# Top-32 attention with two MLPs on one core: leaky ReLU as one parametric ReLU on ScalarE

## The chip, the cores and the metric

The kernel runs on one core of a Trainium2 chip. The metric is device time in microseconds (us), from the first to the last instruction of the program; the median of several executions is given. The engines are TensorE (PE, with PEld for its weight loads), VectorE (DVE), ScalarE (ACT), GpSimd (POOL) and SyncE (SP), which issues most DMAs.

## What is computed

Attention over 4 batches, 8 heads, 576 positions and a head size of 64, in which each query keeps its 32 largest scores; then two MLPs on the 2304 tokens, 512 to 2048 to 512 each. The first one has a leaky ReLU with slope 0.01, the second one a SiLU.

```python
def _moe_ref(x, w_in, w_out):
    h = x @ w_in
    g = np.maximum(0.01 * h, h)
    return (g @ w_out).astype(np.float32)
...
attn_out = _attn_ref(q, k, v)          # softmax over the 32 largest scores of a row
x = attn_out.transpose(0, 2, 1, 3).reshape(B * S, H * D)
x = _moe_ref(x, w_in, w_out)
return _moe2_ref(x, w_in2, w_out2)     # h * sigmoid(h) in place of the leaky ReLU
```

## The kernel before

The 2304 tokens are 18 blocks of 128. Blocks 4 and 13 hold the last 64 tokens of two batches each; the other blocks lie in one batch. A block has four pairs of heads, 72 pairs in all. Everything that a matrix product takes is scaled by a power of two and split into two float16 parts, a high one and a low one (value minus high part), so that a product is three passes of float16.

**Attention**, for each pair: `scores` on PE; `chain`, eight steps for each of two heads on DVE (four MAX8 at lines 479 and 490, three MATCH_REPLACE8 at line 488, and at line 482 a product of the exponentials with the mask, whose two inputs lie in SBUF); `s_copy` and `exps` on ACT (lines 512 and 503); `p_hi` on ACT (517), `p_lo` on POOL (523), `p_transpose` by DMA from SP; `pv` on PE (549). Keys and values of a batch and pair are loaded, scaled and split shortly before the first block that uses them, which is block 0, 4, 9 or 13 (lines 316 to 385).

**The layers**, for each block and layer, in four chunks of 512 columns: `h_quantum` on PE (line 640, 12 matmuls into one of two PSUM tiles); in the first layer `g1_a` on ACT (lines 653 and 654: relu(h), and relu(-0.01 h)) and `g1_b` on POOL (659: the first minus the second); in the second layer `g2_a`, a Tanh on ACT (672), and `g2_b` on DVE (677); then in both `g_hi` on ACT (683), `g_lo` on POOL (688), `g_transpose` by DMA from SP (692), and `o_quantum` on PE (706, 12 matmuls).

**Weights** arrive as 64-bit floats and are decoded to float32 (lines 213 to 232), scaled (261 to 265) and split (275 and 281) while the first blocks run.

**Order.** Each engine works off its instructions in the order of issue. Every step is registered at a position with `at(...)`, 16 positions for a pair of heads, and at the end all steps are issued by position; steps at the same position keep the order in which they were registered. A chunk of layer one has its matmuls at `g1 + QP[i]`, its other steps `OG1` positions later, and `o_quantum` 20 positions later. `OG1` holds the offsets of `g1_a`, `g1_b`, `g_hi`, `g_lo` and `g_transpose`. Within a pair the two exponentials are at positions 8 and 13, the masked products at 14 and 15.

**Buffers.** Tiles of one tag take a fixed number of buffers in turn, and a new tile waits until the last reader of the tile that had its buffer is done. Tag "f" has seven buffers of float32 (loads of q, k and v, both Relu results, Tanh results and others), tag "hl" three for pairs of high and low parts, tag "gT" three for transposed chunks.

Of the kernel before, what the change touches and what calls it, by code (L numbers as in the profile page):

```python
# [14 lines left out]
AF = mybir.ActivationFunctionType  # L15
ALU = mybir.AluOpType
# [2 lines left out]
NEG = -3.0e38  # L19
POS = 16  # L20

# Positions of issue: 16 a pair of heads of a block, relative to the pair's first.
QP = (5, 11, 20, 27)
OK = (-44, -37, -33, -33, -22, -22, -21, -14, -12)
OV = (-5, -2, 7, 11, 13, 15, 17, 25)
# [3 lines left out]
OA = (-7, -20, 7, 5, 8, 13, 17, 17, 23, 28)  # L29
ON = (20, 21, 33, 34, 36, 37)  # L30
OX = (38, 39, 39, 40, 44)
OG1 = (5, 7, 9, 11, 16)
OG2 = (6, 6, 6, 15, 18)
OY = (47, 51, 53, 60, 65)
OO = 52
# [25 lines left out]
def topk_attention_moe_moe2_kernel(  # L61
# [8 lines left out]
    moe2_w_out: bass.AP,  # L70
    out: bass.AP,
):
    """Top-32 attention and two MLPs, as one pipeline over blocks of 128 tokens.

    Every float32 operand of a matrix product is scaled by a power of two, taken from its norm, and
    split into two float16 parts (hi + lo), so that the products run at one pass per pair of parts
    and accumulate in float32.
    """
    nc = tc.nc
    B, H, S, D = q.shape  # L80
    DM = moe_w_in.shape[0]
# [17 lines left out]
    ones = wp.tile([128, 128], F32, name="ones")  # L99
# [4 lines left out]
    w_all = wp.tile([128, (4 * NWP + 1) * 2 * WP], F16, name="w_all")  # L104
# [3 lines left out]
    blocks = []  # L108
# [10 lines left out]
    for s in range(NS):  # L119
        blk, p = divmod(s, NP)  # L120
# [5 lines left out]
    def at(s, p, fn, *args):  # L126
        cal[POS * s + p].append((fn, args))

    def f_tile(shape, name, dt=F32):
        return mp.tile(shape, dt, tag="f", name=name, bufs=NF)  # L130
# [24 lines left out]
        nc.tensor.matmul(out=ps, lhsT=ones, rhs=ss)  # L155
        return ps

# [1 line left out]
    # A pair of chunks is 128 rows of 1024 elements: columns of the first matrix of a layer, two rows  # L159
    # of blocks of the second. Pair c of tensor i ends up as (hi | lo) in slot 8 i + c of w_all. Its  # L160
    # float32 values, before the tensor's norm is known, lie one slot further on, and the float64 ones
    # and the scratch of their decoding in slots that are not used yet.
    w_ss = {}
    w_tmp = {}
    w_bits = [w.bitcast(I32) for w in w_src]
# [21 lines left out]
        return LOAD3[c] if i == 3 and c < 6 else OW[i][0] + OW[i][1] * c  # L187

    def w_rows(i, c, o, n):
        """n elements of each row of pair c, from its element o on, as pairs of 32-bit words."""  # L190
        if i in (0, 2):
            kk, h = divmod(c, DFF // WP)
            o += h * WP
            return w_bits[i][kk * 128:(kk + 1) * 128, 2 * o:2 * (o + n)]
        kk, o = divmod(2 * c * DM + o, DM)
        if n <= DM:
            return w_bits[i][kk * 128:(kk + 1) * 128, 2 * o:2 * (o + n)]
        return w_bits[i][kk * 128:(kk + 2) * 128, :].rearrange("(k p) d -> p k d", p=128)

    def w_load(i, c, o, n):  # L200
        if n == 256:
            t = f_tile([128, 2 * n], "wraw", I32)
        else:
            t = w_raw_at(i, c).bitcast(I32)
        dst = t.rearrange("p (k d) -> p k d", k=2) if n > DM and i % 2 else t
        nc.sync.dma_start(out=dst, in_=w_rows(i, c, o, n))
        w_tmp[i, c, o] = t
# [93 lines left out]
        w_scale["u2"] = a[:, 1:2]  # L301
        w_scale["o"] = a[:, 2:3]

# [1 line left out]
    raw = {}  # L305
    kT = {}
    vt = {}
# [123 lines left out]
        )  # L431
        qT[blk, hf] = t

# [1 line left out]
    st = defaultdict(dict)  # L435

    def scores(s):
# [152 lines left out]
        dst = x_f[blk][:, 256 * hf:256 * hf + 256].rearrange("p (h d) -> p h d", d=D)  # L590
        nc.gpsimd.tensor_tensor(out=dst, in0=st.pop(("t2", blk)), in1=r, op=ALU.mult)

# [1 line left out]
    xs = {}  # L594
    xT = {}
    act_f = {}
# [33 lines left out]
    hp = {}  # L630
    gf = {}
# [15 lines left out]
            del xT["xy"[layer], blk]  # L647

    def g1_a(blk, i):
        t = f_tile([128, 512], "g1p")  # L650
        t2 = f_tile([128, 512], "g1n")
        h = hp.pop((0, blk, i))
        nc.scalar.activation(out=t, in_=h, func=AF.Relu)
        nc.scalar.activation(out=t2, in_=h, func=AF.Relu, scale=-0.01)  # L654
        gf[0, blk, i] = (t, t2)

    def g1_b(blk, i):
        t, t2 = gf[0, blk, i]
        nc.gpsimd.tensor_tensor(out=t, in0=t, in1=t2, op=ALU.subtract)  # L659
        gf[0, blk, i] = t  # L660

    def u2_make(blk):
# [54 lines left out]
        for p0, p1, b, t0 in blocks[blk]:  # L717
            nc.scalar.dma_start(out=out[b * S + t0:b * S + t0 + p1 - p0, :], in_=t[p0:p1])

# [1 line left out]
    at(-5, 0, lambda: nc.vector.memset(ones, 1.0))  # L721
    at(-5, 0, lambda: make_identity(nc, ident))

# [18 lines left out]
    for s in range(NS):  # L742
        blk, p = divmod(s, NP)
# [22 lines left out]
    for blk in range(NB):  # L766
        g1 = G1.get(blk, POS * (NP * blk + 6))
        g2 = G2.get(blk, POS * (NP * blk + 12))
        for i in range(NCH):
            for o, fn in zip(OG1, (g1_a, g1_b)):  # L770
                at(0, g1 + QP[i] + o, fn, blk, i)
            at(0, g1 + QP[i], h_quantum, 0, blk, i)
            at(0, g1 + LAGO[0] + QP[i], o_quantum, 0, blk, i)
            at(0, g2 + QP[i], h_quantum, 1, blk, i)
            for o, fn in zip(OG2, (g2_a, g2_b)):
                at(0, g2 + QP[i] + o, fn, blk, i)
            at(0, g2 + LAGO[1] + QP[i], o_quantum, 1, blk, i)
            for layer, g, og in ((0, g1, OG1), (1, g2, OG2)):
                for o, fn in zip(og[2:], (g_hi, g_lo, g_transpose)):
                    at(0, g + QP[i] + o, fn, layer, blk, i)  # L780
        at(0, g1 + OY[0], y_ready, blk)
        for o, fn in zip(OY, (a_square, a_scales, a_hi, a_lo, a_transpose)):
            at(0, g1 + o, fn, ("y", blk))
        at(0, g2 - 1, u2_make, blk)
        at(0, g2 + OO, o_store, blk)
# [47 lines left out]
```

## Time and profile before

| | |
|---|---|
| median of 3 runs | 1168.95 us (1168.84 to 1169.19) |
| the profiled execution's own time, its span | 1169.7 us |
| busy: PE, DVE, POOL, ACT | 991.2, 1034.7, 846.0, 801.1 us |
| instructions | 18519 |

The profiled execution is one more execution; its time is its span, from the first to the last instruction, and nothing lies around it. Busy times are sums over the whole span, which holds stages of different kinds: decoding of weights at the start, attention and layers side by side, and the last layers alone at the end.

### The profile page before, as it was taken

How to read it: one execution, taken by the hardware profiler on the slowest of the kernel's cores; microseconds unless marked ns; L12 is line 12 of the kernel's file. 1: busy time of each engine (PE TensorE's matmuls, PEld its weight loads, DVE VectorE, ACT ScalarE, POOL GpSimd, SP SyncE). 2: the span in 40 equal slices, each digit the busy share in tenths (PEclk: the TensorE clock that was granted, in tenths of full speed). 3: DMA queues.
4: the chain of work that ended last, by engine and by line, in shares of the span. 5: the costliest groups of instructions: out<-in, count | busy, mean ns of one | idle time of the engine just before them, and what ended most of it. 6: DMA issues, size and time to landing. Idle time of an engine off the chain costs nothing.

```text
span 1169.7 us, 18519 instructions
## 1 busy us (share of the span) xinstructions
PE 991.2 (85%) x6024; PEld 494.6 (42%) x6024; DVE 1034.7 (88%) x2020; ACT 801.1 (68%) x1250; POOL 846.0 (72%) x1097
## 2 busy tenths in 40 slices
PE   2332366378899999999998999999999999999998
PEld 2221233133345544444444444444555444444443
DVE  4999999998999999999999999999999999996000
ACT  7787888787786657576786667577666666574332
POOL 2376788499888877677788777688877777775441
PEclk9555568589999999999999999999999999999999
DMA  9945646534766455564766455566746464664322
GB/s 346 305 130 168 195 146 163 151 73 98 155 143 143 100 117 117 112 135 96 173 158 139 107 118 117 120 146 162 139 92 133 108 143 94 127 119 101 72 64 64
DMA packets 458114, 157.48 MB, mean 135 GB/s; under 512 B 440864, under 2 KB 449056, under 8 KB 455968
## 3 DMA queue, kind: packets, MB, share of 16 engines
q1 hardware_dynamic: 455392, 151.57, 55.2%
q10 hardware_dynamic: 2624, 4.72, 1.2%
q8 instruction: 47, 0.77, 0.3%
q14 instruction: 51, 0.42, 0.1%
HBM read 47.71 MB, written 4.72 MB: 45 GB/s over the span
## 4 chain that ended last, share of the span: by engine, by line
DVE 37%; POOL 17%; PE 15%; issue 15%; ACT 11%; DMA 4%; SPq 1%; POOLq 0%; ACTq 0%; DVEq 0%
DVE w L488 10%; DVE m L490 8%; PE acc L706 7%; DVE e L482 7%; PE h L640 6%; DVE m L479 4%; POOL ph L523 3%; DVE w_all L232 3%; POOL g1p L659 3%; POOL ghl L688 3%; ACT e L503 2%; DVE g2t L677 2%; DVE w_all L220 2%; PE pv L549 1%; POOL w_all L281 1%
## 5 line engine op out<-in xcount | busy, mean ns | idle before, releaser
L706 PE MATMUL acc<-w_all,gT 128*128 128x512 f16 x1728 | 398.0, 380 | 21.1 <-DMA gT<-ghl 9.2
L640 PE MATMUL h<-w_all,xT 128*128 128x512 f16 x1728 | 401.7, 383 | 14.5 <-DMA xT<-xhl 6.3
L490 DVE MAX8 m<-w 128x8 f32<-128x576 f32 x432 | 308.4, 742 | 0.0
L640 PEld LDWEIGHTS <-xT 128*128 128x128 f16 x1728 | 169.8, 99 | 219.8 <-issue 17.3
L706 PEld LDWEIGHTS <-gT 128*128 128x128 f16 x1728 | 164.6, 99 | 215.0 <-issue 17.9
L488 DVE MATCH_REPLACE8 w<-m,w 128x576 f32<-128x576 f32 x288 | 211.1, 738 | 0.0
L523 POOL TENSOR_TENSOR ph<-e,ph 128x1152 f16<-128x1152 f32 x72 | 171.8, 2386 | 24.0 <-ACT ph L517 21.7
L482 DVE SCALAR_TENSOR_TENSOR e<-sb,m,e 128x576 f32<-128x576 f32 x144 | 174.9, 1234 | 3.3 <-ACT e L503 3.3
L659 POOL TENSOR_TENSOR g1p<-g1p,g1n 128x512 f32<-128x512 f32 x72 | 96.7, 1342 | 57.4 <-ACT g1n L654 56.6
L677 DVE SCALAR_TENSOR_TENSOR g2t<-g2t,h 128x512 f32<-128x512 f32 x72 | 48.6, 675 | 94.7 <-ACT g2t L672 93.6
L503 ACT ACTIVATE e<-sb,nb,u 128x576 f32<-128x576 f32 x144 | 120.9, 859 | 5.3 <-POOL nb L495 4.3
L688 POOL TENSOR_TENSOR ghl<-g2t,ghl 128x512 f16<-128x512 f32 x72 | 87.1, 1210 | 47.3 <-ACT ghl L683 47.1
L549 PE MATMUL pv<-vt,pT 128*128 128x128 f16 (+3 forms) x1600 | 112.2, 214 | 9.7 <-DMA pT<-ph 9.7
L688 POOL TENSOR_TENSOR ghl<-g1p,ghl 128x512 f16<-128x512 f32 x72 | 93.9, 1304 | 36.3 <-ACT ghl L683 35.8
L517 ACT ACTIVATE ph<-e 128x1152 f16<-128x1152 f32 x72 | 83.5, 1160 | 51.4 <-DVE e L482 51.4
L241 PE MATMUL gram<-w_all 128*128 128x128 bf16 x256 | 32.4, 292 | 97.6 <-DVE w_all L232 94.6
L683 ACT ACTIVATE ghl<-g1p 128x512 f16<-128x512 f32 x72 | 45.3, 630 | 92.5 <-POOL g1p L659 89.0
L549 PEld LDWEIGHTS <-pT 128*128 128x128 f16 (+3 forms) x1600 | 87.1, 102 | 48.6 <-DMA pT<-ph 11.7
L488 DVE MATCH_REPLACE8 w<-m,S 128x576 f32<-128x576 f32 x144 | 106.2, 743 | 0.0
L479 DVE MAX8 m<-S 128x8 f32<-128x576 f32 x144 | 102.7, 749 | 0.8 <-PE S L448 0.8
L512 ACT ACTIVATE sb<-S 128x1152 f32<-128x1152 f32 x72 | 80.8, 1123 | 31.8 <-DVE w L488 31.7
L448 PE MATMUL S<-kT,qT 128*128 128x64 f16 (+3 forms) x640 | 90.7, 302 | 12.2 <-ACT sb L512 11.7
(94 smaller groups left out, 1242.4 us busy)
## 6 DMA issues: line engine op xcount, KB each, us to landing
w_all<-in_moe_w_in_dram SPq DMA_DIRECT2D x16, 1024.0 KB, 5.4
w_all<-in_moe_w_out_dram SPq DMA_DIRECT2D x14, 1024.0 KB, 5.2
rawk<-in_k_dram SPq DMA_DIRECT2D x16, 256.0 KB, 3.0
rawq<-in_q_dram SPq DMA_DIRECT2D x32, 128.0 KB, 3.0
rawv<-in_v_dram SPq DMA_DIRECT2D x16, 256.0 KB, 3.0
out_dram<-of ACTq DMA_DIRECT2D x16, 256.0 KB, 2.6
gT<-ghl SPq DMA_TRANSPOSE x144, 2.8
wraw<-in_moe_w_out_dram SPq DMA_DIRECT2D x8, 256.0 KB, 3.3
```

The source lines that it names most:

```text
L448: nc.tensor.matmul(out=t[p0:p1, o:o + k1 - k0], lhsT=lhs, rhs=kt[:, k0:k1], start=(x == 0), stop=(x == 1),)
L479: nc.vector.max(m[:, 0], s_ps(s, h))
L482: nc.vector.scalar_tensor_tensor(out=d["e"][:, h], in0=d["sb"][:, h], scalar=m[:, 3, 7:8], in1=d["e"][:, h], op0=ALU.is_ge, op1=ALU.mult, ...
L488: nc.vector.match_replace(w, m[:, step // 2], src, NEG)
L490: nc.vector.max(m[:, step // 2], w)
L503: nc.scalar.activation(out=d["e"][:, h], in_=d["sb"][:, h], func=AF.Exp, scale=d["u"], bias=d["nb"][:, h:h + 1])
L523: nc.gpsimd.tensor_tensor(out=d["ph"][:, 1], in0=d["e"].rearrange("p h k -> p (h k)"), in1=d["ph"][:, 0], op=ALU.subtract)
L549: nc.tensor.matmul(out=o[p0:p1, h, p % 2, 0:n], lhsT=l, rhs=r, start=(i == 0), stop=(i == len(mm) - 1),)
L640: nc.tensor.matmul(out=t, lhsT=a[:, ai], rhs=w_rhs(layer, wi, kk, i), start=(n == 0), stop=(n == 3 * KDM - 1),)
L659: nc.gpsimd.tensor_tensor(out=t, in0=t, in1=t2, op=ALU.subtract)
L688: nc.gpsimd.tensor_tensor(out=n[:, 1], in0=gf.pop((layer, blk, i)), in1=n[:, 0], op=ALU.subtract)
L706: nc.tensor.matmul(out=t, lhsT=g[:, ai], rhs=w_rhs2(layer, wi, 4 * i + j), start=(i == 0 and j == 0 and n == 0), stop=(i == NCH - 1 and j ...
```

## The change

The two Relu passes and the subtraction of a chunk become one pass on ACT, a parametric ReLU with slope (alpha) 0.01, from PSUM to one float32 tile. `g1_b` is gone. The offsets of `g_hi`, `g_lo` and `g_transpose` in the first layer go from 9, 11 and 16 to 7, 9 and 14; the second entry of `OG1` is no longer used. Comments of the file are blanked out, with the line numbers above the change kept.

```diff
-OG1 = (5, 7, 9, 11, 16)
+OG1 = (5, 7, 7, 9, 14)
...
     def g1_a(blk, i):
-        t = f_tile([128, 512], "g1p")
-        t2 = f_tile([128, 512], "g1n")
-        h = hp.pop((0, blk, i))
-        nc.scalar.activation(out=t, in_=h, func=AF.Relu)
-        nc.scalar.activation(out=t2, in_=h, func=AF.Relu, scale=-0.01)
-        gf[0, blk, i] = (t, t2)
-
-    def g1_b(blk, i):
-        t, t2 = gf[0, blk, i]
-        nc.gpsimd.tensor_tensor(out=t, in0=t, in1=t2, op=ALU.subtract)
+        t = f_tile([128, 512], "g1")
+        nc.scalar.activation(out=t, in_=hp.pop((0, blk, i)), func=AF.Prelu, alpha=0.01)
         gf[0, blk, i] = t
...
-            for o, fn in zip(OG1, (g1_a, g1_b)):
+            for o, fn in zip(OG1, (g1_a,)):
                 at(0, g1 + QP[i] + o, fn, blk, i)
```

## Rows read from the trace of the kernel before

**Rows 1.** The page: busy time, share of the span and instructions of each engine.

```profile
PE 991.2 (85%) x6024; PEld 494.6 (42%) x6024; DVE 1034.7 (88%) x2020; ACT 801.1 (68%) x1250; POOL 846.0 (72%) x1097
```

**Rows 2.** Windows by block: length, busy us of PE, PEld, DVE, ACT, POOL, clock, DMA.

```profile
0.00:260.46 260.46, 116.50 (x741) 67.30 (x742) 243.32 (x407) 213.17 (x280) 170.60 (x186) 0.68 0.62 188
260.46:321.83 61.37, 51.12 (x311) 24.44 (x310) 56.47 (x109) 45.69 (x73) 56.30 (x67) 1.00 0.58 123
321.83:378.38 56.55, 54.44 (x376) 28.06 (x375) 52.60 (x115) 41.45 (x72) 49.67 (x74) 1.00 0.63 144
378.38:587.39 209.01, 206.25 (x1263) 101.24 (x1262) 204.82 (x418) 141.35 (x231) 158.96 (x218) 1.00 0.58 122
587.39:646.50 59.11, 53.73 (x316) 26.16 (x315) 56.13 (x116) 42.10 (x74) 49.02 (x70) 0.97 0.66 146
646.50:802.05 155.55, 152.90 (x927) 74.60 (x926) 153.62 (x314) 106.28 (x175) 119.70 (x165) 1.00 0.56 124
802.05:860.82 58.77, 56.12 (x383) 29.07 (x382) 53.59 (x117) 41.67 (x74) 49.64 (x74) 1.00 0.71 146
860.82:1068.96 208.14, 204.66 (x1250) 100.16 (x1249) 204.44 (x416) 135.97 (x218) 154.32 (x205) 1.00 0.54 115
1068.96:1169.70 100.74, 95.52 (x470) 43.57 (x467) 9.68 (x18) 33.42 (x57) 37.76 (x44) 1.00 0.29 69
```

**Rows 3.** The chain of waits from 260 to 322 us.

```profile
by line: issue 21.9%; POOL ph L523 12.5%; POOL ghl L688 9.4%; POOL w_all L281 8.2%; POOL g1p L659 6.0%; DVE w_all L263 4.1%; DVE e L482 3.8%; POOL qnat L423 3.5%; POOL knat L381 2.8%; POOL u L463 2.4%; ACT e L503 2.3%; DVE m L479 2.2%; ACT 
...
266.93 1.23 POOL g1p L659
...
313.93 1.24 POOL g1p L659
```

**Rows 4.** Groups by line: count, busy us, mean ns, idle time before them.

```profile
L659 POOL TENSOR_TENSOR g1p<-g1p,g1n 128x512 f32<-128x512 f32 x72 | 96.7, 1342 | 57.4 <-ACT g1n L654 56.6
...
L672 ACT ACTIVATE g2t<-h,u 128x512 f32<-128x512 f32 x72 | 48.5, 674 | 30.3 <-PE h L640 30.2
L683 ACT ACTIVATE ghl<-g1p 128x512 f16<-128x512 f32 x72 | 45.3, 630 | 92.5 <-POOL g1p L659 89.0 <-DMA gT<-ghl 3.3
...
L654 ACT ACTIVATE g1n<-h 128x512 f32<-128x512 f32 x72 | 42.3, 588 | 0.0
L653 ACT ACTIVATE g1p<-h 128x512 f32<-128x512 f32 x72 | 42.0, 583 | 18.2 <-PE h L640 11.1 <-ACT of L716 3.3 <-issue 2.8
```

**Rows 5.** Waits: us in total, times, longest.

```profile
ACT ghl L683 <- POOL g1p L659: 89.0, 65, 5.0
...
POOL g1p L659 <- ACT g1n L654: 56.6, 32, 5.2
```

**Rows 6.** Windows by block for line 659 alone: length, busy us of POOL.

```profile
0.00:260.46 260.46, 9.51 (x7) 0.68 0.62 188
260.46:321.83 61.37, 5.44 (x5) 1.00 0.58 123
...
587.39:646.50 59.11, 6.91 (x5) 0.97 0.66 146
```

**Rows 7.** Line 482: durations min, median, max in ns; first and last start.

```profile
L482 DVE SCALAR_TENSOR_TENSOR e<-sb,m,e x144: 791/1103/2770, 38.6 to 1069.0; 128x576 f32<-128x576 f32 x144
```

**Rows 8.** Timeline at 913 us: start, us, engine, line.

```profile
913.07 1.27 POOL L659 TENSOR_TENSOR g1p<-g1p,g1n 128x512 f32<-128x512 f32 x1 [1.86 <-ACT g1n L654]
913.54 1.41 DVE L482 SCALAR_TENSOR_TENSOR e<-sb,m,e 128x576 f32<-128x576 f32 x1
```

**Rows 9.** Line 659: durations, first and last start.

```profile
L659 POOL TENSOR_TENSOR g1p<-g1p,g1n x72: 1259/1273/1881, 161.6 to 1116.3; 128x512 f32<-128x512 f32 x72
```

**Rows 10.** Window of the tail, columns as in rows 2.

```profile
1068.96:1130.00 61.04, 61.02 (x312) 28.31 (x310) 5.55 (x12) 23.46 (x42) 29.20 (x36) 1.00 0.31 71
```

**Rows 11.** Waits of the DMA queue on SP.

```profile
SPq L692 <- POOL ghl L688: 112.8, 42, 6.7
```

**Rows 12.** ACT's groups by line: the table load.

```profile
L328 ACT ACT_TABLE_LOAD x1 | 1.3, 1283 | 4.1 <-DMA rawk<-in_k_dram 4.1
```

## The prediction

> **What bounds the kernel now.** I read the page first. VectorE (DVE) is busy 1034.7 us of a span of 1169.7 and PE 991.2, ScalarE (ACT) 801.1 and GpSimd (POOL) 846.0 [rows 1]. By the averages neither ACT nor POOL, the two engines that the change relieves, is the bound. Averages mix stages, so I cut the span by blocks: the boundaries are the starts of the last masked product (line 482) of a block, and blocks of a like kind stand together [rows 2]. Four regimes are to be seen there.
>
> In the first 260 us, blocks 0 to 2, DVE has 243.3 us of work and hardly idles after its first inputs are in; the weights are decoded there and PE is busy 116.5 us only. In block 3, from 260.46 to 321.83, no engine is full: DVE 56.47, PE 51.12, POOL 56.30 of 61.37 us. The chain of waits says which one is late: it runs over POOL from 265 to 315 us, and line 659, the subtraction that goes, has 6.0% of that window of 62 us, which is 3.7 us [rows 3]. From block 4 to 17 PE and DVE are both nearly full: in the stretches of ordinary blocks (the fourth, sixth and eighth row) PE has 206.25 of 209.01, 152.90 of 155.55 and 204.66 of 208.14 us. The two blocks in which keys and values of a new batch come in are looser: block 9 has 59.11 us with PE at 53.73, block 13 has 58.77 with PE at 56.12. After 1068.96 attention is over and PE works off the layers, 95.52 of 100.74 us.
>
> What PE does the change leaves alone, so from block 3 on PE's idle time is what can be won: 10.25 in block 3, 2.11 in block 4, 2.76 + 2.65 + 3.48 = 8.89 in the eleven ordinary blocks, 5.38 in block 9, 2.65 in block 13; together 29.3 us [rows 2].
>
> **What goes.** Of each of the 72 chunks of the first layer the second Relu goes (588 ns, 42.3 us in all) and the subtraction on POOL (1342 ns, 96.7 us). The first pass stays and becomes a parametric ReLU with the operands and the shape of the Relu, 583 ns [rows 4]. That operation is not in this trace. The nearest row is that Relu, with the same input in PSUM and the same output; the Tanh of the same shape with a scale from memory is the farther one, 674 ns [rows 4]. I take 583; at 674 the 72 passes cost 6.6 us more of ACT, which ACT's idle time hides (it is busy 34 to 35 of 52 us in an ordinary block [rows 2]).
>
> ACT also stood still for 89.0 us ahead of the first layer's high parts, until the subtraction was done, and POOL 56.6 us ahead of the subtraction until the second Relu was done [rows 5]. Both waits lose their cause: the high part now follows the ReLU on ACT itself. Late next is the low part on POOL, which waits for the high part as before.
>
> **What that is worth, stage by stage.** The change frees POOL most, so I place its subtraction by stage: 7 of the 72 fall before 260 us with 9.51 us, 5 in block 3 with 5.44, 5 in block 9 with 6.91 [rows 6].
>
> In the first stretch DVE is the bound, and POOL reaches it in one way only. Where a DVE product with both inputs in SBUF meets a tensor operation on POOL, the later of the two waits: at 913.07 us the subtraction starts, and the product of line 482 begun at 913.54 ends with it plus its own work, after 1.41 us where it can be 0.79; over the 144 of them the durations go from 791 to 2770 ns with a median of 1103 [rows 7, 8]. Removing 7 subtractions saves between 0 and 9.5 us there; other POOL work stands in line to collide in their place, so I take 1 us. In block 3 the subtraction is on the chain with 3.7 us; the bounds are 0, if weight conversion on POOL takes the gap, and PE's 10.25. I take 4, the chain's own figure, and a little for the ACT wait behind it. In block 4 I take 1 of 2.11. In block 9 DVE idles 59.11 - 56.13 = 2.98 us, so at about 3 us DVE is the bound there in place of POOL; I take 3 of PE's 5.38. In block 13 I take 1.5 of 2.65. In the eleven ordinary blocks I take 4.5 of 8.89: half, since part of PE's gaps there are starts of matmuls behind transposes and not POOL's doing. The tail gives nothing: PE is busy for 61.02 of 61.04 us up to 1130, beyond the last subtraction, at 1116.3 [rows 9], and its 5.2 idle us lie behind that, in the second layer's last chunks, which the change leaves as they are [rows 10]. For each term 0 is the low end.
>
> **What moves.** High part, low part and transpose of a first-layer chunk are issued two positions earlier (7, 9 and 14 after the chunk's matmuls in place of 9, 11 and 16). On ACT two of four high parts a block thereby pass the second exponential of a pair; they cost 630 ns [rows 4], the second Relu that stood ahead of the same exponential cost 588, so I take nothing. On POOL one low part of four passes the product of line 591; nothing, while POOL has the subtraction's time to give. On SP the transpose is one DMA a chunk. In ordinary blocks it passes no other DMA. In the blocks that load keys and values it passes loads of both, and while it waits for its low part they wait behind it: 42 such waits, of both layers, now hold SP 112.8 us, 2.7 us each [rows 11]. I take nothing, since low parts come 1.3 us earlier by the subtraction that is gone; if that cover fails, it is a rival below. The buffers help: a chunk takes one of the seven float32 buffers in place of two. The three buffers of the high and low parts are taken two positions earlier and given back two positions earlier, so they are held no longer.
>
> **The sum.** 1 + 4 + 1 + 3 + 1.5 + 4.5 = 15 us. Against the profiled execution, whose own time is its span of 1169.7, that gives 1154.7; the median of the runs, 1168.95, lies 0.75 below it, so 1154. A measurement of this kernel can tell some 0.2%, 2.3 us, from no change.
>
> **Rivals.** 1. *Everything is won*: the freed POOL and ACT close PE's gaps from block 3 on, all 29.3 us, or most of them and a few us of the first stretch. For it: the subtraction alone is 96.7 us of POOL. Against it: PE also waits for transposes and for DVE. About 1140 to 1146.
>
> 2. *PE and DVE are full anyway*: in the ordinary blocks PE's gaps stay, in block 3 weight conversion fills the hole, and in the blocks with loads the transposes hold up the loads by 2.7 us each and eat the 5.5 us taken for blocks 4, 9 and 13. For it: PE is at 98 to 99% in most of the body [rows 2]. Left are at most a few us: 1165 to 1169, say 1168. With more loads held up (three blocks by 2.7 us and no gain) it would be 1173, slower.
>
> 3. *Table switches, slower.* ACT's functions come from tables; the trace has one load of a table, 1283 ns, for everything that the kernel uses now [rows 12]. If the parametric ReLU is in no table with the exponential, each of the 72 stands between two exponentials of a pair or of neighbouring pairs and needs a load before it and one after it: 144 x 1.283 = 184.8 us, and ACT goes from 801.1 to about 944 us. That still fits under the span, so the price is what of it stands ahead of DVE's products and PE's chunks; at two loads a block on the path it is 18 x 2.57 = 46 us, and with the 15 won, 1200. It decides as soon as one load a block is on the path (23 us against 15). For it: the function is new to this kernel. Against it: Square, Copy, Relu, Exp and Tanh all live in the table loaded once, and a variant of Relu may well be beside them. The Trainium skill ("ScalarE: Activation LUTs", What ACT_TABLE_LOAD costs) counts a drain with each switch, 2.66 us in all; by that 144 switches would be an estimated 383 us, ACT would have some 1142 us of work and be the bound, at over 1200 us; the trace has the load's 1283 ns, and no run shows the drain.
>
> That the operation gives another slope than 0.01 is possible too; it would take the same time, so it is no case of its own here.
>
> **How the numbers follow.** The forecast's mechanism, POOL's relief in block 3 and in the blocks with loads and half of the small gaps, gets 0.57 (1147 to 1164); rival 1 gets 0.15; rival 2 gets 0.16 near no change and 0.04 on the slower side; the table switches get 0.08. Faster is 0.57 + 0.15 and a hundredth of rival 2: 0.73; same 0.15; slower 0.04 + 0.08 = 0.12. The range is 1140, where PE's gaps from block 3 on are all closed (1168.95 - 29.3 = 1139.7), to 1171, which takes in rival 2 near no change; outside are the table switches, the slower side of rival 2, and a few hundredths below.
>
> **What would show it.** Right: ACT has 72 passes of about 580 ns in the first layer and no more than one table load; POOL's busy time is near 750 us; no wait of the high part for POOL; block 3 is shorter by about 4 us, block 9 by about 3, ordinary blocks by 0.4 each, the tail as long as now. Wrong: PE's idle time from block 3 to 17 still near 29 us, or far less than 14; table loads by the dozen; SP's waits for low parts longer, with the loads of blocks 9 and 13 later than now; the gain, if any, in the first 260 us.

## The result, and the profile after

| | before | after |
|---|---|---|
| median of 4 runs | 1169.07 us (1168.84 to 1170.45) | 1157.67 us (1155.61 to 1158.98) |
| ratio, 95% interval | 1 | 0.9895 [0.9881, 0.9909] |
| span of the profiled execution | 1169.7 us | 1155.9 us |

The change makes the kernel 1.05% faster, 11.4 us. The forecast was 1154.

The runs after the change list a span beside each time, and 1.8 us lie around it (1157.73 and 1155.9 for the profiled one). The statement ahead of the prediction that the own time of the profiled execution is its span was therefore not exact: with the same 1.8 us, the execution that was profiled before took an estimated 1171.5, 2.4 above its median. So 2.4 of the 13.8 us between the two spans lie between that one execution and the median of its four, and 11.4 are the change as measured. In the runs below the kernel before has medians of 1171.07 to 1171.46 and single executions from 1168.92 to 1172.99, so 2 us either way stay open in what one span or one set of four says.

The page of the kernel after, busy time by engine, answers to [rows 1]:

```profile
PE 992.4 (86%) x6024; PEld 496.1 (43%) x6024; DVE 1012.9 (88%) x2020; ACT 764.4 (66%) x1178; POOL 746.7 (65%) x1025
```

POOL lost 99.3 us and ACT 36.7, as the removed instructions say. DVE, on whose instructions the change does nothing, lost 21.8 us as well. That is the first thing to explain.

The windows by block of the kernel after, with the columns of [rows 2] and the same boundaries (last start of line 482 in a block); here block 5 (fourth row) and blocks 6 to 8 (fifth row) stand apart, which are one row, the fourth, in [rows 2]:

```profile
0.00:260.23 260.23, 118.75 (x762) 68.81 (x763) 241.44 (x407) 210.19 (x274) 166.17 (x181) 0.76 0.66 189
260.23:322.32 62.09, 52.07 (x291) 24.15 (x289) 52.23 (x109) 43.99 (x69) 47.13 (x61) 0.95 0.51 119
322.32:381.50 59.18, 55.05 (x373) 28.34 (x372) 52.95 (x117) 39.41 (x68) 42.82 (x69) 0.98 0.62 139
381.50:436.37 54.87, 54.87 (x349) 27.29 (x348) 50.66 (x106) 32.56 (x52) 35.51 (x52) 0.99 0.52 112
436.37:586.37 150.00, 150.00 (x909) 73.61 (x908) 149.25 (x315) 99.22 (x160) 101.66 (x149) 1.00 0.62 128
586.37:643.52 57.15, 55.90 (x335) 27.68 (x334) 53.61 (x117) 40.87 (x71) 43.41 (x66) 1.00 0.70 153
643.52:794.68 151.16, 149.81 (x914) 73.17 (x913) 149.40 (x314) 99.29 (x162) 102.43 (x152) 1.00 0.60 127
794.68:849.71 55.03, 54.95 (x377) 28.40 (x376) 53.13 (x116) 40.64 (x71) 44.90 (x70) 1.00 0.71 157
849.71:1055.14 205.43, 205.43 (x1258) 101.02 (x1257) 200.51 (x418) 127.07 (x201) 132.71 (x189) 1.00 0.56 116
1055.14:1155.90 100.76, 95.56 (x470) 43.63 (x468) 9.67 (x18) 31.21 (x51) 29.92 (x38) 0.99 0.29 69
```

Two halves with opposite signs are to be seen. From block 6 on, PE is full (150.00 of 150.00, 205.43 of 205.43) and the blocks are shorter. In blocks 3 and 4 nothing is full, and they are longer than before. I split the span at the end of block 5 and use three names from here on: the **start** (blocks 0 to 5), the **body** (blocks 6 to 17) and the **tail**. The body in one row, first the kernel before:

```profile
432.97:1068.96 635.99, 619.32 (x3786) 304.05 (x3784) 621.38 (x1273) 432.30 (x713) 490.48 (x673) 1.00 0.58 125
```

and the kernel after:

```profile
436.37:1055.14 618.77, 616.08 (x3787) 303.89 (x3786) 605.91 (x1275) 407.08 (x664) 425.11 (x625) 1.00 0.61 129
```

So the start lost 3.4 us (432.97 to 436.37), the body won 17.2, and the tail stayed (100.74 and 100.76). Of the 16.7 us in which PE stood still in the body, 2.7 are left.

DVE's body has 15.5 us less of work. One line accounts for nearly all of it, the masked product; before, in the groups by line of the body:

```profile
L482 DVE SCALAR_TENSOR_TENSOR e<-sb,m,e 128x576 f32<-128x576 f32 x97 | 116.3, 1220 | 2.8 <-ACT e L503 2.8
```

and after:

```profile
L482 DVE SCALAR_TENSOR_TENSOR e<-sb,m,e 128x576 f32<-128x576 f32 x98 | 101.9, 1063 | 0.6 <-ACT e L503 0.6
```

The same products take 14.4 us less. The prediction saw one of them end behind the subtraction [rows 8], and the median of all 144 went from 1103 ns [rows 7] to 813, near the shortest (791). The trace shows the cause product by product. Of the 96 that start in the body before, 54 take over 900 ns, and 53 of these end 611 to 619 ns after the end of the POOL instruction that was running when they began; the other 42 take 791 to 844 ns. After, 46 of 47 long ones end in the same way. What the long ones take above 791 ns is 40.6 us before and 26.0 after: what DVE lost here was waiting for POOL. The Trainium skill ("SBUF — State Buffer", SBUF: two separate sides) says that a DVE instruction with two SBUF inputs and a GpSimd instruction that reads SBUF exclude each other, each for its whole length. Those ends agree with it. The runs below agree too: the mean of this line over the body is 1037 to 1096 ns in the kernels without POOL's load there, and 1196 to 1241 in those with it. All else that DVE does in the body is 503 to 505 us, before, after and in every run without added DVE work.

### The profile page after: what moved, and what is told of

Its sections match the earlier page's. It is cut to its first block, busy times and chain, and to the rows that moved or that the text cites. A ratio compares the mean times of both kernels' runs of the same rounds, so it can differ in the third digit from the quotient of the medians.

```text
span 1155.9 us, 18357 instructions
## 1 busy us (share of the span) xinstructions
PE 992.4 (86%) x6024; PEld 496.1 (43%) x6024; DVE 1012.9 (88%) x2020; ACT 764.4 (66%) x1178; POOL 746.7 (65%) x1025
## 5 line engine op out<-in xcount | busy, mean ns | idle before, releaser
L482 DVE SCALAR_TENSOR_TENSOR e<-sb,m,e 128x576 f32<-128x576 f32 x144 | 154.0, 1090 | 1.8 <-ACT e L503 1.8
L680 POOL TENSOR_TENSOR ghl<-g,ghl 128x512 f16<-128x512 f32 x72 | 87.4, 1215 | 67.0 <-ACT ghl L675 42.5
L448 PE MATMUL S<-kT,qT 128*128 128x64 f16 (+3 forms) x640 | 93.4, 306 | 18.7 <-ACT sb L512 18.3
L512 ACT ACTIVATE sb<-S 128x1152 f32<-128x1152 f32 x72 | 80.9, 1123 | 21.9 <-DVE w L488 21.8
L281 POOL TENSOR_TENSOR w_all<-w_all 128x1024 f16<-128x1024 f32 x32 | 71.6, 2238 | 12.0 <-ACT w_all L275 10.6
L664 ACT ACTIVATE g2t<-h,u 128x512 f32<-128x512 f32 x72 | 48.7, 676 | 43.1 <-PE h L640 43.1
```

The source lines that it names most:

```text
L448: nc.tensor.matmul(out=t[p0:p1, o:o + k1 - k0], lhsT=lhs, rhs=kt[:, k0:k1], start=(x == 0), stop=(x == 1),)
L482: nc.vector.scalar_tensor_tensor(out=d["e"][:, h], in0=d["sb"][:, h], scalar=m[:, 3, 7:8], in1=d["e"][:, h], op0=ALU.is_ge, op1=ALU.mult, ...
L680: nc.gpsimd.tensor_tensor(out=n[:, 1], in0=gf.pop((layer, blk, i)), in1=n[:, 0], op=ALU.subtract)
```

## The experiments

The theory after the result had three parts: the body's gain comes from POOL's load that is gone; not from the waits of ACT that went with it, nor from the second ReLU pass; and the start's loss comes from the order of instructions there. The rivals were the link (ACT's wait for POOL), the ACT pass, the offsets, and DVE's time alone. The float32 buffers that the change frees are a further one; e5 and e6 below take one buffer a chunk, as after, and lose the gain all the same. All runs are in one table. "Start" is the end of block 5 against 432.97; start and body are from one profile each. The bodies repeat well: 617.4 to 619.3 us in the seven kernels with neither POOL's load there nor pads, 635.7 to 636.4 in the three with the old subtraction. The starts are less sure: the profiled executions of e1, e8 and e10 took 1.8 to 2.2 us more than the medians of their runs, and that much of their starts may be the execution's.

| run | median | ratio, interval | start | body |
|---|---|---|---|---|
| before | 1169.07 | 1 | 0 | 635.99 |
| after | 1157.67 | 0.9895 [0.9881, 0.9909] | +3.4 | 618.77 |
| e1 old offsets | 1158.06 | 0.9889 [0.9870, 0.9907] | +6.5 | 618.18 |
| e2 free load on POOL | 1247.27 | 1.0649 [1.0633, 1.0664] | +92.1 | 619.34 |
| e3 link through POOL | 1159.33 | 0.9897 [0.9880, 0.9915] | +5.6 | 618.91 |
| e4 second ACT pass | 1153.07 | 0.9844 [0.9829, 0.9858] | -2.6 | 618.59 |
| e5 load, no link | 1189.51 | 1.0159 [1.0145, 1.0173] | +14.4 | 639.62 |
| e6 load and link | 1182.53 | 1.0098 [1.0085, 1.0112] | +8.2 | 637.44 |
| e7 blocks 0-3 old, rest new | 1151.54 | 0.9837 [0.9823, 0.9852] | -0.1 | 617.36 |
| e8 before, new offsets | 1183.26 | 1.0108 [1.0094, 1.0122] | +13.6 | 636.37 |
| e9 two DVE pads | 1157.04 | 0.9895 [0.9878, 0.9911] | +0.1 | 621.33 |
| e10 blocks 0-3 new, rest old | 1176.08 | 1.0052 [1.0039, 1.0065] | +6.9 | 635.66 |
| e11 second pass, blocks 0-3 | 1152.61 | 0.9845 [0.9832, 0.9859] | +0.1 | 617.71 |
| e12 four DVE pads | 1182.74 | 1.0096 [1.0079, 1.0113] | +16.5 | 632.01 |

The other times of the kernel before, on the chips of these runs, were 1171.07 to 1171.46.

### e1: the change without its new offsets

```diff
-OG1 = (5, 7, 7, 9, 14)
+OG1 = (5, 7, 9, 11, 16)
```

> The changed kernel with the first layer's offsets back at 9, 11 and 16 for high part, low part and transpose; the parametric ReLU stays. Theory (the freed POOL and ACT time is what counts, the offsets only follow): 1157 to 1160 us, within 2 us of the changed kernel. Rival (the earlier issue is what counts): 1163 to 1168 us, most of the 11 us lost.

1158.06 us, the same as after and in the theory's range. Its body row:

```profile
439.52:1057.70 618.18, 615.49 (x3787) 303.56 (x3786) 606.14 (x1273) 406.79 (x664) 424.57 (x625) 1.00 0.62 129
```

The body has its whole gain with the old offsets: moving the high part, low part and transpose forward gives nothing there.

### e2: a load on POOL that nothing depends on

```diff
+    scr = wp.tile([128, 176], F32, name="scr")
...
+    def g1_b(blk, i):
+        for _ in range(3):
+            nc.gpsimd.tensor_tensor(out=scr, in0=scr, in1=scr, op=ALU.subtract)
...
+            for o, fn in zip(OG1, (g1_a, g1_b)):
```

> The changed kernel with POOL's load put back without its place in the chain: in each chunk's place of the subtraction POOL subtracts a scratch tile from itself, 3 x 128x176 float32, about 1.3 us, and nobody waits for the result. Theory (POOL's time and its collisions with DVE are what counts): 1164 to 1168 us, POOL busy again near 845 us, DVE's line 482 back from 154 to about 170 us. Rival (ACT's wait for POOL in the middle of the chunk is what counts): 1157 to 1160 us although POOL is as busy as before.

1247.27 us, far outside every expectation, and not for the reason that was to be tested. The windows of the added line alone (length, busy us of POOL, clock, DMA):

```profile
0.00:50.00 50.00, 31.16 (x54) 0.90 0.87 289
50.00:100.00 50.00, 39.17 (x78) 0.50 0.00 0
100.00:150.00 50.00, 35.98 (x66) 0.50 0.39 101
150.00:200.00 50.00, 9.74 (x21) 0.53 0.55 164
200.00:300.00 100.00, 0.00 (x0) 0.65 0.59 151
```

All 216 pieces ran in the first 200 us, before nearly all the chunks that they were issued with. In this program, what waits for nothing is laid earlier on its engine: the position at which a step is registered does not fix its place. The statement ahead of the prediction that all steps are issued by position is therefore not the whole of it. In the start the pieces held up POOL's other work: from 39.6 to 70.1 us POOL ran nothing but pieces, and ACT waited up to 34.2 us for a bias of the exponentials (line 496), with its part of the decoding of weights behind that. The start grew by 92 us. The run says nothing on a load in the body; as the body has none, its 619.34 us is one more body without POOL's load. It also shows that an added step need not stay where it was registered.

### e3: the link without the load

```diff
+    def g1_b(blk, i):
+        t = gf[0, blk, i]
+        nc.gpsimd.tensor_scalar(t[:, 0:1], t[:, 0:1], 1.0, None, op0=ALU.mult)
...
+            for o, fn in zip(OG1, (g1_a, g1_b)):
```

> The changed kernel with the link through POOL put back without its load: between the ReLU and the high part POOL multiplies one column of the tile by 1 (128x1, about 0.25 us, 18 us in all), and ACT waits for it. Theory (POOL's time counts): 1157 to 1161 us, with the wait of the high part for POOL back at 50 to 80 us. Rival (ACT's wait counts): 1164 to 1168 us.

A POOL operation of one column stands between ReLU and high part. 1159.33 us is in the theory's range. The list of waits shows the link back, in half of its old size ([rows 5] have 89.0) and a little under what was expected:

```profile
ACT ghl L679 <- POOL g L656: 47.1, 38, 5.5
```

and the body in spite of it:

```profile
438.57:1057.48 618.91, 615.96 (x3785) 303.38 (x3783) 608.77 (x1273) 406.81 (x664) 434.00 (x673) 1.00 0.62 129
```

47.1 us of waits of ACT are worth 0.1 us of the body. The 89.0 us in [rows 5] look by this like waits of an engine that had time; the other half of them was not put back.

### e4: the second pass on ACT without the load

```diff
+        h = hp.pop((0, blk, i))
-        nc.scalar.activation(out=t, in_=hp.pop((0, blk, i)), func=AF.Prelu, alpha=0.01)
+        nc.scalar.activation(out=t, in_=h, func=AF.Prelu, alpha=0.01)
+        nc.scalar.activation(out=junk[:, 0:512], in_=h, func=AF.Relu, scale=-0.01)
```

> The changed kernel with the second Relu pass back on ACT (128x512 from PSUM, about 0.59 us, 42 us in all), its result unused. Theory (ACT has room, POOL's time counts): 1157 to 1160 us, ACT busy 807 us. Rival (ACT's load or the later release of the PSUM tile counts): 1162 to 1167 us.

```profile
430.36:1048.95 618.59, 615.59 (x3784) 303.39 (x3783) 607.49 (x1275) 428.12 (x712) 425.62 (x625) 1.00 0.62 129
```

The row above is the body: ACT has 428.12 us of work, nearly what it had before (432.30), and the length is that of after. The pass that the change took from ACT is worth nothing in the body. The kernel with this useless pass is even faster than after, 1153.07 us, below both expected ranges, because its start is 6.0 us shorter (430.36 against 436.37).

### e5: the load without the link

```diff
+    scr = wp.tile([128, 176], F32, name="scr")
...
+        t = gf[0, blk, i]
+        for o, n in ((0, 172), (172, 172), (344, 168)):
+            nc.gpsimd.tensor_tensor(out=scr[:, 0:n], in0=t[:, o:o + n], in1=scr[:, 0:n], op=ALU.subtract)
...
+            for o, fn in zip(OG1, (g1_a, g1_b)):
```

> The changed kernel with POOL's load put back at its place in each chunk: after the ReLU POOL subtracts the chunk's tile from a scratch tile in three pieces of 172, 172 and 168 columns, about 1.3 us a chunk, and nobody waits for the result; the high part does not wait for POOL. Theory (POOL's time and its collisions with DVE in the body are what counts): 1164 to 1169 us, with the 17 us lost that all versions without this load win behind block 5. Rival (load and wait together are needed): 1156 to 1160 us.

The pieces read the ReLU's result, so they can't be laid earlier than it, and nobody waits for them. Their group, and then the body by engine and for line 483 (the masked product, 482 before):

```profile
L658 POOL TENSOR_TENSOR scr<-g,scr 128x172 f32<-128x172 f32 (+1 forms) x216 | 129.6, 600 | 51.0 <-ACT g L652 39.4
```

```profile
447.42:1087.04 639.62, 618.56 (x3786) 303.91 (x3785) 620.47 (x1273) 405.50 (x664) 508.32 (x769) 1.00 0.68 125
```

```profile
L483 DVE SCALAR_TENSOR_TENSOR e<-sb,m,e 128x576 f32<-128x576 f32 x97 | 116.5, 1223 | 2.5 <-ACT e L504 2.5
```

A load with no link takes the whole gain back, and 3.6 us more; at 129.6 us it is also larger than the old subtraction (96.7). DVE's work and line 483 are back at their old figures (621.38 and 116.3 before) although DVE's instructions are unchanged. The products wait little for the pieces themselves: in the body 10 of 67 long products began during a piece, with 2.8 us above 791 ns in all, and 21 during a low part of the first layer, with 17.0 us (after: 18, with 7.5). Here the load acts mostly by moving POOL's later work onto the products; in the kernel before, 14 began during the subtraction itself, with 10.5 us, and 15 during the low part, with 12.8. The median, 1189.51, missed both expectations, and by the start: 14.4 us that they had not.

### e6: load and link, without the second pass

```diff
+    scr = wp.tile([128, 1], F32, name="scr")
...
+        t = gf[0, blk, i]
+        nc.gpsimd.tensor_tensor(out=t, in0=t, in1=scr.to_broadcast([128, 512]), op=ALU.subtract)
...
+            for o, fn in zip(OG1, (g1_a, g1_b)):
```

> The changed kernel with load and link through POOL both back: after the ReLU POOL subtracts a zero from the whole tile in place (128x512, about 1.27 us), and the high part waits for it; only the second Relu pass of the kernel before is missing. Both theories: 1165 to 1171 us, near the kernel before. Rival (the second pass on ACT carries a part of the gain): 1158 to 1163 us.

The body, and the wait for POOL from the list of waits:

```profile
441.20:1078.64 637.44, 620.62 (x3786) 303.62 (x3784) 622.51 (x1275) 407.45 (x664) 478.72 (x674) 1.00 0.68 125
```

```profile
ACT ghl L680 <- POOL g L657: 95.8, 66, 6.7
```

With 79.5 us of POOL work in place of 96.7 the body is 1.5 us from before's. The median, 1182.53, lies above both expected ranges, again by the start (8.2 us). The loads of e5 and e6 differ in size, so the two do not price the link beside a load. With e3 they settle the body all the same: the load does it with and without the link, and the link does nothing without the load.

### e7 and e10: the two halves apart

e7 has the two passes, the subtraction and the old offsets in blocks 0 to 3, and the change from block 4 on; e10 is the reverse. The edit of e7, against the kernel before (e10 has `<` in place of `>=`):

```diff
+OG1P = (5, 7, 7, 9, 14)
+HYB = 4
...
     def g1_a(blk, i):
+        if blk >= HYB:
+            t = f_tile([128, 512], "g1")
+            nc.scalar.activation(out=t, in_=hp.pop((0, blk, i)), func=AF.Prelu, alpha=0.01)
+            gf[0, blk, i] = t
+            return
...
     def g1_b(blk, i):
+        if blk >= HYB:
+            return
...
-            for layer, g, og in ((0, g1, OG1), (1, g2, OG2)):
+            for layer, g, og in ((0, g1, OG1P if blk >= HYB else OG1), (1, g2, OG2)):
```

> Blocks 0 to 3 as in the kernel before (two Relu passes and the subtraction, offsets 9, 11, 16), blocks 4 to 17 as in the changed kernel. Theory (the body's gain behind block 5 is 17 us whatever the start does, and the 3 us lost up to block 5 come from the order of the start's work being laid out anew): 1151 to 1154 us, block 5 ending within 1.5 us of the kernel before. Rival (POOL's relief helps the start and is masked by something else): 1157 us or more.

Blocks 0 to 2, block 3 and the body of e7:

```profile
0.00:260.57 260.57, 116.89 (x741) 67.61 (x742) 243.44 (x407) 213.24 (x280) 171.17 (x186) 0.67 0.62 188
260.57:321.93 61.36, 52.66 (x311) 24.94 (x310) 57.81 (x108) 45.92 (x73) 56.14 (x67) 0.97 0.56 122
432.86:1050.22 617.36, 615.37 (x3787) 303.91 (x3786) 604.82 (x1273) 407.22 (x664) 425.22 (x625) 1.00 0.62 129
```

Block 3 is as long as before (61.37) and POOL has nearly the same work in it; the body has the whole gain. At 1151.54 us, in the theory's range, this is the lowest median of the study, below before and after with intervals that lie apart from after's (0.9852 against 0.9881).

> Blocks 0 to 3 as in the changed kernel, blocks 4 to 17 as in the kernel before: the reverse of the hybrid. Theory (start and body add up, the start of the changed kernel is 2 to 4 us longer, the body as before): 1171 to 1176 us, the body from block 5's end 636 us. Rival (the relief in the start is felt later): below 1168 us.

Block 3 and the body of e10:

```profile
260.96:324.48 63.52, 51.85 (x295) 24.49 (x293) 52.15 (x111) 43.93 (x69) 47.43 (x61) 0.95 0.52 116
...
439.85:1075.51 635.66, 618.94 (x3786) 303.92 (x3784) 618.44 (x1273) 431.71 (x713) 493.09 (x673) 1.00 0.58 125
```

The change in blocks 0 to 3 alone makes the kernel 0.5% slower, at 1176.08 us just above the theory's range: block 3 takes 63.52 us, in an execution 2.1 us above the median, PE's mean granted clock there is 0.95 as in after, and the body gains nothing.

### e8: the new offsets on the kernel before

```diff
-OG1 = (5, 7, 9, 11, 16)
+OG1 = (5, 7, 7, 9, 14)
```

> The kernel before with the changed kernel's offsets 7, 9 and 14 for high part, low part and transpose; both Relu passes and the subtraction stay. Theory (offsets do not count): 1167 to 1172 us. Rival: below 1165 us.

With `g1_b` still at 7, the high part now stands at the same position as the subtraction. The body:

```profile
446.58:1082.95 636.37, 617.68 (x3786) 303.69 (x3784) 620.58 (x1275) 431.93 (x713) 491.42 (x673) 1.00 0.59 125
```

In the body the offsets do nothing (0.4 us), as e1 says from the other side. In the start they cost 13.6 us, and the median, 1183.26, lies outside both expectations. With the single pass the new offsets are not worse there than the old ones (3.4 against 6.5 us lost, the latter in an execution 2.2 us above its median).

### e9 and e12: DVE's time given back without POOL

Pads of one column on DVE, issued ahead of every masked product, two in e9 and four in e12, were to give DVE its old work without any of POOL's.

```diff
+            for _ in range(2):
+                nc.vector.tensor_scalar(m[:, 1, 0:1], m[:, 1, 0:1], 1.0, None, op0=ALU.mult)
```

> The changed kernel with two small operations more on DVE ahead of each masked product (128x1, in place, times 1), POOL as in the changed kernel. From block 5's end to block 17's end the kernel before had 116.3 us of line 482 on DVE and the changed one 101.9; the pads put about 0.15 to 0.2 us a product back, 15 to 20 us in the body's 97 products. Theory (POOL's load cost the body through DVE's waits for POOL, DVE's time is what counts): the body is 10 to 18 us longer than the changed kernel's 618.8, the whole 1167 to 1177 us, POOL as idle as in the changed kernel. Rival (POOL's lateness counts, not DVE's time): the body within 4 us of 618.8, the whole 1157 to 1162 us.

The body of e9, and its pads in the groups by line of the body:

```profile
433.03:1054.36 621.33, 616.04 (x3786) 303.16 (x3784) 614.28 (x1466) 406.39 (x664) 418.21 (x625) 1.00 0.61 128
```

```profile
L483 DVE TENSOR_SCALAR m<-m 128x1 f32<-128x1 f32 x194 | 23.6, 138 | 0.0
```

194 pads of 138 ns are 23.6 us in their own row, but DVE's busy time rose by 8.4 only, 43 ns a pad; the rest overlaps its neighbours in the records. So e9 gave back half of what it was meant to, and the body grew by 2.6 us. 1157.04 us and this body lie where the rival put them, but with half the DVE work that both expectations took, the run does not decide between them.

> The changed kernel with four small operations more on DVE ahead of each masked product; two of them put 8.4 us on DVE in the body (605.9 to 614.3) and made the body 2.6 us longer (618.8 to 621.3), so four should put about 17 us there and bring DVE to some 622 us of work, what it had in the kernel before (621.4). Theory (DVE's time is what POOL's load cost the body): the body 630 to 637 us, the whole 1167 to 1173 us. Rival (the waits that POOL's lateness makes on other engines are the larger part): the body 622 to 628 us, the whole 1158 to 1165 us.

The body of e12, with four pads:

```profile
449.51:1081.52 632.01, 617.57 (x3786) 303.53 (x3785) 628.21 (x1659) 405.01 (x662) 418.29 (x625) 1.00 0.59 126
```

This time DVE has 628.2 us, more than before (621.4), and is the bound: 3.8 us of idle time are left of 632.0. The body is in the range of the theory, but with 6 us more DVE work than the expectation took; the whole, 1182.74, is above both ranges, by a start that is 16.5 us longer. The body lies 4 us below before's although DVE has 7 us more work. Between e9 and e12, at before's 621.4 us, the body would be about 621.33 + 10.68 x 7.10 / 13.93 = 626.8 us. By that interpolation, DVE's time accounts for some 8 of the 17.2 us. From after over e9 to e12 each us of DVE costs more than the one before it, so a straight line puts that part rather too high. The other 9 are put down to POOL being late by argument; no run isolates them, and a run with just 621.4 us of DVE work was not made. What the runs show is that neither part alone is the whole: e12 has more DVE work than before and a shorter body, and e9 a longer body than after with POOL as in after.

### e11: the second pass in blocks 0 to 3 alone

```diff
+        if blk < 4:
+            nc.scalar.activation(out=junk[:, 0:512], in_=h, func=AF.Relu, scale=-0.01)
```

> The changed kernel with the second Relu pass, its result unused, in blocks 0 to 3 only: the start of the version that had the pass in all blocks (2.6 us ahead of the kernel before at block 5's end) and the changed kernel's body. Theory (start and body add up): 1150 to 1153 us, block 5 ending 1 to 4 us ahead of the kernel before. Rival (that start was luck of one execution): 1156 to 1158 us.

1152.61 us, in the theory's range and 5 us less than after by adding a pass whose result nobody reads. In the two profiles 3.3 us of that lie in the start (433.08 against 436.37 to the end of block 5) and 1.1 in the body, which is as in the other kernels without the load:

```profile
433.08:1050.79 617.71, 615.29 (x3787) 303.75 (x3786) 604.29 (x1275) 407.18 (x664) 426.22 (x625) 1.00 0.62 129
```

Block 5 ends 0.1 us behind the kernel before, and not ahead of it as expected. Block 3 of this run:

```profile
263.88:321.10 57.22, 49.21 (x289) 23.37 (x288) 53.23 (x107) 45.44 (x73) 48.90 (x62) 1.00 0.59 128
```

It is 4.1 us shorter than before, and in e4, too (57.27): without the subtraction block 3 can have the forecast gain. But blocks 0 to 2 end 3.4 us later here (263.88 against 260.46), and block 4 is some 2 to 3 us longer than before in both runs. e4, e7 and e11 can't be told apart by their intervals.

### What the start shows

A stretch of the order of ACT's instructions in block 1, as the two traces have it; lines 653, 654 and 683 of before are 651 and 675 of after:

```
before:  L683 g_hi, L213 decode, L517 p_hi, L653, L654, L575, L512 s_copy, L683 g_hi, L503
after:   L675 g_hi, L265 scale,  L517 p_hi, L651,       L575, L675 g_hi, L512 s_copy, L213 decode, L503
```

The decoding of a weight (line 213) has moved behind a copy of scores, a scaling (265) ahead of both, and neither line is touched by the diff. What follows from such an order is seen in block 3 of the kernel after, in its timeline (start, us, engine, line; in brackets the idle time ahead and its releaser):

```profile
282.99 2.12 POOL L281 TENSOR_TENSOR w_all<-w_all 128x1024 f16<-128x1024 f32 x1
...
285.14 1.06 ACT L275 ACTIVATE w_all<-w_all 128x1024 f16<-128x1024 f32 x1 [2.27 <-POOL w_all L281]
...
286.10 1.11 ACT L512 ACTIVATE sb<-S 128x1152 f32<-128x1152 f32 x1
...
287.27 2.08 PE L448 MATMUL S<-kT,qT 128*128 128x512 f16 x8 [5.75 <-ACT sb L512]
```

ACT waits for POOL's split of a weight, the copy of scores stands behind it in ACT's queue, and PE, whose next scores go where the copy reads, stands still for 5.75 us. In the kernel before, the same scores waited 1.41 us for their copy:

```profile
283.28 1.14 PE L448 MATMUL S<-kT,qT 128*128 128x512 f16 x8 [1.41 <-ACT sb L512]
```

The eight matmuls take 1.14 us there and 2.08 us behind the long standstill. The granted clock was 1.00 (2.4 GHz) up to 286 us and is 0.50 (1.2 GHz) just behind the standstill. Two windows of the kernel after, the first just behind it and the second of 280 to 320 us:

```profile
288.00:290.00 2.00, 2.00 (x9) 0.75 (x8) 0.02 (x1) 1.24 (x3) 2.00 (x3) 0.50 0.40 91
280.00:320.00 40.00, 31.99 (x180) 14.81 (x180) 33.07 (x72) 27.96 (x48) 31.71 (x44) 0.91 0.57 133
```

and 280 to 320 us before:

```profile
280.00:320.00 40.00, 31.56 (x190) 15.12 (x189) 37.68 (x76) 28.97 (x50) 35.34 (x47) 1.00 0.72 146
```

PE has 180 matmuls in place of 190, in about the same busy time, at a mean granted clock of 0.91 in place of 1.00 (a mean between the two levels). This one wait is longer, but not all waits together: over the whole of block 3 PE stands still for 10.02 us after and 10.25 before, and what PE does there takes 52.07 us for 291 matmuls in place of 51.12 for 311. Over the thirteen changed kernels the start moves by -2.6 to +16.5 us, and by +92.1 in e2, also by edits that the body does not feel (e1, e3, e4, e8). Why each one's start comes out as it does was not settled; that it is the order and not the work is argued from e4 and e11, where added work makes the start shorter.

## Why the prediction was right, and where its steps failed

| stage | forecast gain | measured, by the two profiles |
|---|---|---|
| 0 to 260 us | 1 | 0.2 |
| block 3 | 4 | -0.7 |
| block 4 | 1 | -2.6 |
| block 9 | 3 | 2.0 |
| block 13 | 1.5 | 3.7 |
| eleven ordinary blocks | 4.5 | 11.2 |
| tail | 0 | 0.0 |
| sum | 15 | 13.8 |

**The parts of the change** came as costed. The parametric ReLU takes a Relu's time, 587 ns for the 583 taken, and ACT still loads one table; in ACT's groups by line of the kernel after:

```profile
L675 ACT ACTIVATE ghl<-g 128x512 f16<-128x512 f32 x72 | 45.1, 627 | 4.5 <-DMA gT<-ghl 2.1 <-DMA kT<-knat 0.9 <-POOL knat L381 0.2
L651 ACT ACTIVATE g<-h 128x512 f32<-128x512 f32 x72 | 42.3, 587 | 32.0 <-PE h L640 29.9 <-ACT of L708 1.7
L328 ACT ACT_TABLE_LOAD x1 | 1.3, 1283 | 3.9 <-DMA rawk<-in_k_dram 3.9
```

The rival of table switches falls by the last line, which is that of [rows 12]. The 92.5 us of idle time ahead of the high part [rows 4] are 4.5 now. POOL's 746.7 us is the 750 that was named.

**The sum** is 13.8 us by the profiles where 15 was forecast, but its terms are not right: those of blocks 3, 4 and 9 were too high, those of block 13 and of the ordinary blocks too low, and they made up for each other: that the sum came out so near is luck. The forecast of 1154 lies 3.7 below the median: 1.2 from the sum, and 2.4 because by that much the profiled execution of before lies above the median.

**The step that failed is block 3**, "I take 4, the chain's own figure". The low bound named beside it, that weight conversion on POOL takes the gap, is the nearer one, and even that was too kind. The subtraction was on the chain in that block, but without it weight work, scores and chunks stand in another order on ACT, POOL and DVE, and PE waits as long for others (10.02 us for 10.25), as for the split and the copy in the timeline above. e10 repeats it: the change in blocks 0 to 3 alone gives a block 3 of 63.52 us. e4 and e11, with one more pass on ACT and so another order, have the 4.1 us; a step's share of the chain did not say which order would come. Block 4 lost 2.6 us where 1 was to be won; its own waits were not followed. Behind both stands "What moves", which took the rest of the order as it was and its cost as nothing. The two earlier positions themselves do not explain the 3.4 us lost by the end of block 5: with the old ones (e1) the start is no shorter. Which of the other moves does was not settled.

**The term that was mis-sized is the eleven ordinary blocks**, 4.5 for 11.2 us. There PE was expected to keep half of its gaps. It closed nearly all of them: the stretch of blocks 6 to 8 has PE busy for 150.00 of 150.00 us. The collisions of line 482 with POOL were seen and counted in the first 260 us only, at 1 us; in the body a good third of that waiting went, and it is worth 14.4 us of DVE. The reading of [rows 8] was a little off, too: the product ends 0.61 us behind the subtraction (914.95 and 914.34), as nearly all long ones do, and not its own 0.79. The prediction's rule, that PE's idle time is what can be won, held: 14.0 of the body's 16.7 us of PE idle went, and the rest of the 17.2 is PE's own records (619.3 to 616.1 us).

**Rivals.** "Everything is won" is what happened in the body; with the start as it was it gives e7, 1151.5, above its 1140 to 1146, since block 3 and 4 held 12.4 of its 29.3 us. "PE and DVE are full anyway" fails in the body: DVE was full in part with waiting for POOL, which its busy time does not tell. SP's waits for low parts did grow, a sign that the prediction named as one of being wrong (112.8 us in 42 waits [rows 11]); after:

```profile
SPq L684 <- POOL ghl L680: 133.3, 48, 6.6
```

The cost that this rival put on them (2.7 us a block with loads) did not come: blocks 9 and 13 are 2.0 and 3.7 us shorter.

## What to carry to other kernels

Work taken from an engine that is not the bound can still shorten the bound's own instructions: compare the durations of one instruction, minimum and median, before counting an engine as full, and price the collisions in every stage where they occur. Do not price a step by its share in a chain where other work of the same engine stands ready behind it. Where the order within a stage is laid anew at each edit, judge an edit by stage, and keep its parts only in the stages where it pays: here blocks 4 to 17 with the new form and blocks 0 to 3 with the old one, 1151.5 us. Two versions with the new form everywhere and a useless pass in the start (e4 and e11) cannot be told apart from it, so this is one order that suits the start and not the only one.

## What the runs showed of the hardware

- Of the masked products (128x576, two SBUF inputs) that took over 900 ns in the body, 53 of 54 before and 46 of 47 after ended 611 to 619 ns after the end of the POOL instruction that was running when they began.
- The masked product takes 791 ns at its shortest, and 1220 on average beside 490 us of POOL work in the body, 1063 beside 425. The gain on DVE, 14.4 us, is more than a fifth of the 65.4 us that POOL lost there.
- A parametric ReLU on ACT with its slope given in the instruction costs 587 ns from PSUM at 128x512, against 583 for a Relu, and needs no table beside that of exponential, Tanh, Square and Copy.
- A DVE operation on one column has a record of 138 to 140 ns, but two of them ahead of each product cost DVE's busy time 43 ns each (e9: 8.4 us for 194), and four 58 (e12: 22.3 us for 386).
- POOL's subtraction of 128x512 took 1342 ns with two full inputs [rows 4], and 1104 on average where the second input is one column repeated (e6: 79.5 us for 72).
